# Handing a part of the row stores and relays of a long convolution from SyncE's queue to GpSimd's

## The chip, the cores and the metric

The kernel runs on one core of a Trainium2 chip. The metric is the device time of one execution in microseconds; the time before is 187.96 us, the median of three runs (187.35 to 188.18). All durations below come from one execution taken by the hardware profiler, whose span from the first to the last instruction is 187.3 us.

## The reference

Two independent heads read sequences of 2048 steps and 640 channels in bf16, and their results are laid side by side in an output of 2048 x 1280.

Head A is a diagonal complex state space model. Each channel pair turns x into 640 complex states by a matrix B, runs a recurrence over time, and maps back by a matrix C; a skip term x * Dskip is added:

```
h = Lam_bar * h + Bu[t]            # 2048 steps, 640 complex states
y = 2 * real(h @ C.T) + x * Dskip
```

Head B is a long convolution. k is first convolved with a kernel of 4 taps per channel and multiplied by v; the product kv is convolved over the whole sequence with a kernel of 2048 taps per channel, by Fourier transforms of length 4096; then a skip and a gate by q:

```
kv = conv4(k, shift_k) * v
y  = irfft(rfft(kv) * rfft(ssm_k))[:2048] + kv * ssm_D
out_B = q * y
```

## The kernel before

The program is a list of operations, each with the engines that may run it, a function that issues it, and the memory that it writes and reads. From those footprints `depend` (L92) finds what each operation must wait for. A long string, `ORDER` (L1117), fixes the rest: each entry such as `388S0` names operation 388, the engine that runs it (A ScalarE, V VectorE, G GpSimd, T TensorE, S SyncE), and a PSUM bank. `emit` (L122) issues the operations in that order; each engine runs its own in the order in which the string names them, and an operation at the head of an engine's queue that must wait holds all behind it. SyncE (SP) issues nearly all DMAs; ScalarE issues a few at the start; GpSimd issues none.

Head A works on TensorE with matmuls that fold 16 steps into one coarse step (L581, L602), a scan on VectorE (`coarse`, L656, with its multiplications on L679 and L682 to L690), matmuls that unfold again (L225 and L229, evicted on L726 and L728), and the map by C with the skip term (`project`, L732). The skip multiplies rows of x by `DR`, a copy of Dskip on all 128 partitions. `ld_Dr` (L372), which loads it, is the 91st operation; its first reader is `xd0` (L737).

Head B does its transforms as small matmuls. The channels are worked in five blocks of 128 for the short convolution, and in two halves of 320 for the long one. For block d:

- `load_kv` (L811) loads k and v of the block transposed, channels on partitions (L814). There is one k buffer (KT) for all five blocks, so `ld_k2` waits until the last tap of block 1 has read KT, `ld_k3` until the last tap of block 2, and so on; v has three buffers.
- `conv` (L827) multiplies k by the taps (L205 on VectorE, L206 on ScalarE), adds (L840) and multiplies by v (L841). All of blocks 0 to 2 but a few taps is on VectorE; the last product of block 3 is GpSimd's next work after the set-up tables.
- `plane` (L843) stores the 128 finished rows of 4096 bytes to a scratch tensor in DRAM, `kv_rows`: operations `pl0` to `pl4`.
- `relay` (L850) reads the rows of a half back with the 32 x 64 split of time that the transform needs. There are eight pieces a half, each of 40 channels: 32 partitions x 40 rows x 128 bytes, so 1280 separate runs of 128 bytes. A piece waits for the stores that hold its 40 channels.
- `s1` (L860, matmuls on L876 and L881, evicted on L886) is the first transform stage over the relayed rows; its units 0 to 4 read the four pieces of the first 40 columns, units 5 to 9 the other four. The second stage is on L900 and L913.

SP's order around the change is: the loads of k and v for blocks 0 and 1 and parts of x, the first load of C, `ld_k2`, `pl0`, `ld_v2`, a second load of C, `pl1`, `ld_k3`, the first piece, `pl2`, then the other seven pieces with two small loads among them, `ld_v3`, rows of x, `ld_k4`, a third part of C, the four loads of the second half's long kernel (L807), `ld_Dr`, and more rows of x.

Of the kernel before, what the change touches and what calls it, by code (L numbers as in the profile page):

```python
# [20 lines left out]
PACT, PDVE, PPOOL, PPE, PSP = "A", "V", "G", "T", "S"  # L21
# [336 lines left out]
def params(c):  # L358

    P, nc, v, f = c.P, c.nc, c.v, c.f  # L360
    V, G, A = PDVE, PPOOL, PACT
    lam_re, lam_im, ldt_in, dsk_in = c.ins["A_Lambda_re"], c.ins["A_Lambda_im"], c.ins["A_log_dt"], c.ins["A_Dskip"]
# [3 lines left out]
    for k, src in enumerate((lam_re, lam_im, ldt_in)):  # L366
        rows = pr[10 * k:10 * k + 10, :]
        P.add("ld_par", {PSP: .1, PACT: .1}, lambda e, rows=rows, src=src: e.dma_start(
            out=rows.rearrange("p (a b) -> p a b", a=2), in_=bass.AP(src.tensor, 0, [[64, 10], [0, 2], [1, 64]])),
            outs=[tk[:, k:k + 1]], ins=[pr], nbytes=2560)  # L370
    c.DR = v("DR")
    P.add("ld_Dr", {PSP: .1}, lambda e: e.dma_start(out=c.DR, in_=bass.AP(dsk_in.tensor, 0, [[0, 128], [1, 640]])), outs=[c.DR],  # L372
          nbytes=128 * 1280)
    PV = v("PV").bitcast(f32)
    g = P.group(1)
# [11 lines left out]
    for i, n in enumerate((1, 2, 4, 8, 16)):  # L387
        P.add("rn", {A: .2}, lambda e, i=i, n=n: e.activation(out=rn[:, i, :], in_=rho, func=FN.Exp, scale=float(n)),
              outs=[rn[:, i, :]], ins=[rho])
# [17 lines left out]
    for i in range(1, 4):  # L407
        P.add("fn", {G: .2}, lambda e, i=i: e.tensor_tensor(out=fn[:, i, :], in0=fn[:, i - 1, :], in1=fn[:, i - 1, :], op=ALU.add),
              outs=[fn[:, i, :]], ins=[fn[:, i - 1, :]])
    P.add("ph", {G: .4}, lambda e: e.tensor_tensor(  # L410
        out=ph.rearrange("p (x m) -> p x m", m=2), in0=bc(fn.rearrange("p n j -> p (n j)").rearrange("p (x o) -> p x o", o=1), [128, 40, 2]),
# [5 lines left out]
        out=al3, in0=al3, in1=bc(rn[:, 0:4, :].rearrange("p n j -> p (n j)").rearrange("p (x o) -> p x o", o=1), [128, 40, 2]), op=ALU.mult),  # L417
        outs=[al], ins=[al, rn[:, 0:4, :]])
# [4 lines left out]
    for lo, mi, val in ((0, 0, 1.0), (0, 1, 0.0), (64, 0, 0.0), (64, 1, 1.0)):  # L423
# [17 lines left out]
          outs=[t3(ga)[:, :, 0]], ins=[t3(ma)[:, :, 0], t3(mb)[:, :, 1]])  # L441
# [28 lines left out]
    for x in range(2):  # L470
# [5 lines left out]
              outs=[pc], ins=[ps, c30])  # L476
# [291 lines left out]
class PartB:  # L768
# [74 lines left out]
    def plane(self, d):  # L843

        c, P = self.c, self.c.P
        vt, tok = c.v("VT", 2048 * (d % 3), 2048), c.tok[:, d:d + 1]
        P.add(f"pl{d}", {PSP: 1.6}, lambda e: e.dma_start(out=c.kvdram[128 * d:128 * d + 128, :], in_=vt), outs=[tok], ins=[vt],
              nbytes=128 * 4096)

    def relay(self, hf):  # L850

        c, P = self.c, self.c.P
        for x, gh in [(x, gh) for gh in range(2) for x in range(4)]:
            lo = 320 * hf + 80 * x + 40 * gh
            dst = self.KV[32 * x:32 * x + 32, 40 * gh:40 * gh + 40]
            src = c.kvdram[lo:lo + 40, :].rearrange("n (a b) -> a n b", b=64)
            P.add(f"rl{hf}_{x}{gh}", {PSP: 1.2}, lambda e, dst=dst, src=src: e.dma_start(out=dst, in_=src), outs=[dst],
                  ins=[c.tok[:, lo // 128:(lo + 39) // 128 + 1]], nbytes=40 * 4096)

    def s1(self, what, hf, u):  # L860
# [237 lines left out]
def plain_order(P):  # L1098
# [16 lines left out]


ORDER = (  # L1117
# [40 lines left out]
)  # L1158


# [68 lines left out]
```

## Time and profile before

| what | value |
|---|---|
| median of three runs | 187.96 us |
| span of the profiled execution | 187.3 us |
| time of the runs less the span of the profile | about 0.7 us |
| TensorE (PE) busy | 175.6 us, 94% of the span |
| VectorE (DVE) busy | 158.0 us, 84% |
| ScalarE (ACT) busy | 147.7 us, 79% |
| GpSimd (POOL) busy | 72.6 us, 39% |
| granted TensorE clock | 0.999 |
| DMA | 30.15 MB in 106682 packets, 101274 of them under 512 bytes |

The profile's page does not print a time of the profiled execution beside its span; the sums below are made against the span of 187.3 us, and the 0.7 us around it are added at the end. In timeline rows the first number is the start in microseconds, the second the duration of the whole row, then the engine, the line and the operation, written and read tensor, shape, and the number of instructions merged into the row. Square brackets hold the idle time of that engine before the row and what ended it. An SP row lasts as long as SyncE needed to hand the DMA over, not until the data has landed.

### The profile page before, as it was taken

The numbers are of one execution on the slowest core, as the hardware profiler recorded it, in microseconds if no ns is written. First come the engines' busy times: TensorE is split into PE (matmuls) and PEld (weight loads), VectorE is DVE, ScalarE is ACT, GpSimd is POOL, SyncE is SP. The second block draws the span as 40 slices with busy tenths as digits, with TensorE's granted clock in tenths as the row PEclk, the third lists the DMA queues.
The fourth block names the chain that finished last, engine by engine and source line by source line (L and its number), as shares of the span: only waits on it lengthen the run. The fifth ranks groups of instructions, "written<-read, shape, count | busy, mean of one in ns | idle before, by whom it ended". The sixth has DMA issues, their size and how long they took to land.

```text
span 187.3 us, 7665 instructions
## 1 busy us (share of the span) xinstructions
PE 175.6 (94%) x3398; PEld 126.3 (67%) x3399; DVE 158.0 (84%) x225; ACT 147.7 (79%) x181; POOL 72.6 (39%) x68
## 2 busy tenths in 40 slices
PE   7998999999799979979997999999999999999992
PEld 2565666677468756656685688776588876887770
DVE  3537964679959899999969999899999999998961
ACT  2469699989899979999997997997898883985000
POOL 8679999900000000008803925730740000551620
PEclk9999999999999999999999999999999999999999
DMA  5999999799999989999989479402496993058996
GB/s 153 191 184 158 200 143 140 141 174 182 198 253 154 290 179 152 180 182 154 138 109 251 154 170 133 75 5 72 122 196 120 210 227 85 15 160 187 208 219 173
DMA packets 106682, 30.15 MB, mean 161 GB/s; under 512 B 101274, under 2 KB 106010, under 8 KB 106650
## 3 DMA queue, kind: packets, MB, share of 16 engines
q1 hardware_dynamic: 106332, 29.35, 86.7%
q8 instruction: 26, 0.43, 1.1%
q10 hardware_dynamic: 318, 0.33, 0.6%
q14 instruction: 6, 0.05, 0.1%
HBM read 11.32 MB, written 7.86 MB: 102 GB/s over the span
## 4 chain that ended last, share of the span: by engine, by line
PE 54%; DVE 23%; DMA 9%; ACT 8%; issue 3%; DVEq 0%; ACTq 0%
PE acc L225 17%; PE acc L581 13%; DMA arena<-in_B_k_dram 9%; PE acc L229 6%; DVE arena L728 6%; PE acc L900 6%; DVE arena L205 5%; ACT arena L913 5%; PE acc L951 4%; DVE arena L840 3%; PE acc L972 3%; PE acc L539 2%; DVE arena L754 2%; PE acc L881 1%; ACT arena L886 1%
## 5 line engine op out<-in xcount | busy, mean ns | idle before, releaser
L581 PE MATMUL acc<-arena 128*64 128x512 bf16 x400 | 45.6, 380 | 1.8 <-DVE arena L457 1.1
L913 ACT CAST arena<-acc 128x960 bf16<-128x960 f32 (+1 forms) x43 | 37.4, 916 | 4.0 <-PE acc L900 2.2
L225 PE MATMUL acc<-arena 128*128 128x320 bf16 (+2 forms) x255 | 36.4, 297 | 2.2 <-DVE arena L754 1.1
L581 PEld LDWEIGHTS <-arena 128*64 128x64 bf16 x400 | 26.0, 110 | 17.8 <-DVE arena L457 1.3
L886 ACT CAST arena<-acc 128x1024 bf16<-128x1024 f32 x37 | 35.8, 1034 | 2.1 <-PE acc L881 2.0
L225 PEld LDWEIGHTS <-arena 128*128 128x128 bf16 x256 | 23.7, 98 | 12.1 <-DVE arena L754 1.3
L841 POOL TENSOR_TENSOR arena<-arena 128x2048 bf16<-128x2048 bf16 x2 | 8.8, 4410 | 53.7 <-DVE arena L840 46.1
L900 PE MATMUL acc<-arena 128*64 128x160 bf16 x512 | 23.6, 235 | 1.8 <-DVE arena L679 1.4
L900 PEld LDWEIGHTS <-arena 128*64 128x64 bf16 x512 | 18.6, 110 | 8.3 <-ACT arena L913 2.2
L229 PE MATMUL acc<-arena 128*64 128x320 bf16 (+3 forms) x258 | 23.2, 313 | 0.5 <-DVE arena L690 0.5
L840 DVE TENSOR_TENSOR arena<-arena 128x2048 bf16<-128x2048 bf16 x14 | 17.6, 1256 | 4.5 <-ACT arena L206 4.3
L728 DVE TENSOR_TENSOR arena<-acc,arena 128x1024 bf16<-128x1024 f32 (+2 forms) x19 | 20.4, 1114 | 0.9 <-PE acc L229 0.5
L760 POOL TENSOR_TENSOR arena<-arena 128x640 bf16<-128x640 f32 x3 | 4.2, 1416 | 32.6 <-ACT arena L752 32.6
L956 ACT CAST arena<-acc 128x1024 bf16<-128x1024 f32 x16 | 15.4, 1025 | 1.7 <-PE acc L951 1.6
L229 PEld LDWEIGHTS <-arena 128*64 128x64 bf16 x258 | 13.0, 110 | 3.5 <-DVE arena L690 0.6
L876 PE MATMUL acc<-arena 128*64 128x128 bf16 x400 | 14.6, 220 | 0.2 <-ACT arena L886 0.2
L876 PEld LDWEIGHTS <-arena 128*64 128x64 bf16 x400 | 12.9, 110 | 2.4 <-ACT arena L886 0.9
L205 DVE TENSOR_SCALAR arena<-arena 128x2048 bf16<-128x2048 bf16 x15 | 11.0, 749 | 3.6 <-DMA arena<-in_B_k_dram 3.5
L754 DVE TENSOR_TENSOR arena<-acc,arena 128x640 bf16<-128x640 f32 x13 | 10.7, 820 | 3.5 <-PE acc L225 2.2
L206 ACT ACTIVATE arena<-arena 128x2048 bf16<-128x2048 bf16 (+2 forms) x10 | 11.1, 1112 | 1.5 <-DMA arena<-in_B_k_dram 1.5
L924 DVE TENSOR_TENSOR arena<-arena 128x2560 bf16<-128x2560 bf16 x8 | 11.9, 1484 | 0.1
L602 PE MATMUL acc<-arena 128*64 128x256 bf16 (+2 forms) x140 | 11.6, 291 | 0.1
(142 smaller groups left out, 284.4 us busy)
## 6 DMA issues: line engine op xcount, KB each, us to landing
out_dram<-arena SPq DMA_DIRECT2D x32, 160.0 KB, 3.3
arena<-in_B_ssm_k_dram SPq DMA_DIRECT2D x8, 320.0 KB, 6.1
kv_rows<-arena SPq DMA_DIRECT2D x5, 512.0 KB, 4.7
arena<-kv_rows SPq DMA_DIRECT2D x16, 160.0 KB, 4.0
arena<-in_A_x_dram SPq DMA_DIRECT2D x16, 160.0 KB, 3.5
arena<-in_B_q_dram SPq DMA_DIRECT2D x8, 320.0 KB, 6.3
arena<-in_A_B_im_dram ACTq DMA_DIRECT2D x1, 160.0 KB, 2.8
arena<-in_A_B_re_dram SPq DMA_DIRECT2D x1, 160.0 KB, 3.0
```

The lines of the kernel that those rows point to most:

```text
L205: vm = lambda e: lambda out, in_, by: e.tensor_scalar_mul(out=out, in0=in_, scalar1=by)
L225: e.matmul(out, lhsT=lhsT, rhs=rhs, start=start, stop=stop, skip_group_check=True)
L229: e.matmul(out[half], lhsT=lhsT[:, half], rhs=rhs, start=start, stop=stop, skip_group_check=True, tile_position=(0, 64 * r))
L581: e.matmul(o[64 * r:64 * r + 64], lhsT=self.BT[j][:, r, d, :], rhs=self.XP[:, d, 2 * q:2 * q + 2], start=(d == 0), stop=(d == 4), skip_gro ...
L728: e.tensor_tensor(out=o, in0=b, in1=o, op=ALU.add)
L754: e.tensor_tensor(out=two(ys), in0=two(B)[:, :, 0:320], in1=two(ys), op=ALU.add)
L840: P.add(f"ca{d}_{j}", tt, lambda e: e.tensor_tensor(out=t1, in0=t1, in1=t2, op=ALU.add), outs=[t1], ins=[t1, t2])
L876: e.matmul(B[64 * b:64 * b + 64, 128 * i:128 * i + 128], lhsT=lh[i], rhs=F[:, b, :], start=True, stop=True, tile_position=(0, 64 * b))
L886: P.add(f"e1{what}{hf}_{u}", {PACT: act(1024), PDVE: dve(1024)}, lambda e, B: c.CP[e](out=out, in_=(B.rearrange("p (l n s k) -> p k s l n" ...
L900: e.matmul(B[64 * s:64 * s + 64, 512 * b + 160 * i:512 * b + 160 * i + 160], lhsT=c.W[:, k, 64 * b:64 * b + 64], rhs=self.AS[hf][:, k, 160 ...
L913: c.CP[e](out=out, in_=b.rearrange("p r (k j n) -> p r k j n", k=n, j=4) if nj > 1 else b.rearrange("p r (k x) -> p r k x", k=n))
L956: P.add(f"er2{hf}_{u}", {PACT: act(1024), PDVE: dve(1024)}, lambda e, B: c.CP[e](out=out, in_=B.rearrange("p (s n b) -> p b s n", s=2, n=4 ...
```

## The change

Nine DMAs get GpSimd as their issuer: the stores `pl0` and `pl1` of the first two blocks, the load of Dskip `ld_Dr`, and six of the eight relay pieces of the first half (`rl0_00`, `rl0_01`, `rl0_10`, `rl0_11`, `rl0_20`, `rl0_21`). `pl2` and the two pieces that read block 2 (`rl0_30`, `rl0_31`) stay on SP. On GpSimd the nine stand between the last set-up product (84) and the last product of block 3 (453), in the order pl0, ld_Dr, pl1, rl0_00, rl0_01, rl0_10, rl0_11, rl0_20, rl0_21. In the string `388G0 91G0` stand right behind the end of block 0's convolution (387), and the other seven right behind the end of block 1's (398). The order of everything else, on every engine, is unchanged.

The diff, with the string cut to the entries that move:

```
-    P.add("ld_Dr", {PSP: .1}, ...
+    P.add("ld_Dr", {PSP: .1, PPOOL: .1}, ...
-        P.add(f"pl{d}", {PSP: 1.6}, ...
+        P.add(f"pl{d}", {PSP: 1.6, PPOOL: 1.6}, ...
-            P.add(f"rl{hf}_{x}{gh}", {PSP: 1.2}, ...
+            P.add(f"rl{hf}_{x}{gh}", {PSP: 1.2, PPOOL: 1.2}, ...
...
-  84G0 387V0 201T4 ... 400S0 ... 81A0 388S0 64V0 ... 398V0 199T0 ... 232A4 399S0 407V0
-  ... 243T6 411S0 207T0 ... 208A0 415S0 236A4 ... 414S0 ... 416S0 321V0 413S0 ... 412S0 ... 417S0 ... 91S0
+  84G0 387V0 388G0 91G0 201T4 ... 400S0 ... 81A0 64V0 ... 398V0 399G0 411G0 415G0 412G0 416G0 413G0 417G0 199T0
+  ... 232A4 407V0 ... 243T6 207T0 ... 208A0 236A4 ... 414S0 ... 321V0 ...
```

More of the change, by code (lines that the diff above doesn't have):

```diff
@@ L371, in params @@
     c.DR = v("DR")
-    P.add("ld_Dr", {PSP: .1}, lambda e: e.dma_start(out=c.DR, in_=bass.AP(dsk_in.tensor, 0, [[0, 128], [1, 640]])), outs=[c.DR],
+    P.add("ld_Dr", {PSP: .1, PPOOL: .1}, lambda e: e.dma_start(out=c.DR, in_=bass.AP(dsk_in.tensor, 0, [[0, 128], [1, 640]])), outs=[c.DR],
           nbytes=128 * 1280)
@@ L846, in plane @@
         vt, tok = c.v("VT", 2048 * (d % 3), 2048), c.tok[:, d:d + 1]
-        P.add(f"pl{d}", {PSP: 1.6}, lambda e: e.dma_start(out=c.kvdram[128 * d:128 * d + 128, :], in_=vt), outs=[tok], ins=[vt],
+        P.add(f"pl{d}", {PSP: 1.6, PPOOL: 1.6}, lambda e: e.dma_start(out=c.kvdram[128 * d:128 * d + 128, :], in_=vt), outs=[tok], ins=[vt],
               nbytes=128 * 4096)
@@ L856, in relay @@
             src = c.kvdram[lo:lo + 40, :].rearrange("n (a b) -> a n b", b=64)
-            P.add(f"rl{hf}_{x}{gh}", {PSP: 1.2}, lambda e, dst=dst, src=src: e.dma_start(out=dst, in_=src), outs=[dst],
+            P.add(f"rl{hf}_{x}{gh}", {PSP: 1.2, PPOOL: 1.2}, lambda e, dst=dst, src=src: e.dma_start(out=dst, in_=src), outs=[dst],
                   ins=[c.tok[:, lo // 128:(lo + 39) // 128 + 1]], nbytes=40 * 4096)
```

78 rows, old and new, of the table ORDER are left out of this document.

## The prediction

> **What bounds the kernel now.** I read the page first, then the chain of waits in order of time, then the timelines of SP, PE, DVE and POOL around the moved DMAs.
>
> ```profile
> span 187.3 us, 7665 instructions
> ...
> PE 175.6 (94%) x3398; PEld 126.3 (67%) x3399; DVE 158.0 (84%) x225; ACT 147.7 (79%) x181; POOL 72.6 (39%) x68
> ...
> DMA  5999999799999989999989479402496993058996
> ```
>
> PE is without work for 11.7 us of the span, so a change of issue can win little; it can lose much, since every engine runs a fixed order. The slices show the DMA engines nearly always busy from 5 to 100 us, which is where all nine moved DMAs lie. The chain, in order of time (start, duration):
>
> ```profile
> 34.99 6.07 DMA arena<-in_B_k_dram
> ...
> 48.18 5.76 DMA arena<-in_B_k_dram
> ...
> 59.81 5.37 DMA arena<-in_B_k_dram
> ...
> 65.20 1.42 DVE arena L205 x2
> 66.62 0.74 DVE arena L679
> ...
> 67.41 0.61 PE acc L900 x12
> ```
>
> Three of its links are flights of k (blocks 1, 2, 3): a k lands, DVE convolves it, the one k buffer comes free, the next k is issued. The last landing reaches PE by DVE's fixed order: two taps of block 3, then L679, which frees PE. PE and DVE show that as waits:
>
> ```profile
> 53.96 0.75 DVE L205 TENSOR_SCALAR arena<-arena 128x2048 bf16<-128x2048 bf16 x1 [1.90 <-DMA arena<-in_B_k_dram]
> ...
> 58.84 0.75 DVE L205 TENSOR_SCALAR arena<-arena 128x2048 bf16<-128x2048 bf16 x1
> ...
> 64.49 0.07 DVE L668 MEMSET arena<- 128x10 f32 x1
> 65.20 1.42 DVE L205 TENSOR_SCALAR arena<-arena 128x2048 bf16<-128x2048 bf16 x2 [0.65 <-DMA arena<-in_B_k_dram]
> ```
> ```profile
> 67.41 0.61 PE L900 MATMUL acc<-arena 128*64 128x160 bf16 x12 [1.39 <-DVE arena L679]
> ```
>
> **What SP shows.** Its queue over the same time:
>
> ```profile
> 48.18 2.14 SPq L814 DMA_TRANSPOSE arena<-in_B_k_dram  x1
> 50.37 0.58 SPq L847 DMA_DIRECT2D kv_rows<-arena  x1
> 51.00 3.93 SPq L814 DMA_TRANSPOSE arena<-in_B_v_dram  x1
> 54.97 3.23 SPq L556 DMA_TRANSPOSE arena<-in_A_C_im_dram  x1
> 58.30 1.40 SPq L847 DMA_DIRECT2D kv_rows<-arena  x1
> 59.81 3.06 SPq L814 DMA_TRANSPOSE arena<-in_B_k_dram  x1
> 63.04 0.46 SPq L857 DMA_DIRECT2D arena<-kv_rows  x1
> ...
> 67.63 3.23 SPq L857 DMA_DIRECT2D arena<-kv_rows  x4
> ...
> 72.74 1.86 SPq L857 DMA_DIRECT2D arena<-kv_rows  x2
> ...
> 77.68 0.53 SPq L736 DMA_DIRECT2D arena<-in_A_x_dram  x1
> ...
> 90.58 3.45 SPq L372 DMA_DIRECT2D arena<-in_A_Dskip_dram  x1
> ```
>
> SP is never free between 48.18 and 63.04, but equal stores take 0.58 and 1.40 us of it, and the load of Dskip, as large as a block of rows of x that takes 0.53, takes 3.45 behind four large loads. So an issue lasts not as long as its own work but until the engines have taken what stands ahead: SP is slow because the DMA engines are full. What the change takes off SP is then still to be carried by the same engines, and some of it earlier than now.
>
> **The change, part by part.**
>
> 1. The two stores. `pl0` waits for block 0's product, `pl1` for block 1's; the first ends at 37.89 + 1.23 = 39.12, the second at 50.83 + 1.23 = 52.06, and POOL has nothing to do from 37.88:
>
> ```profile
> 37.89 1.23 DVE L841 TENSOR_TENSOR arena<-arena 128x2048 bf16<-128x2048 bf16 x1 [1.83 <-DMA arena<-in_B_v_dram]
> ...
> 50.83 1.23 DVE L841 TENSOR_TENSOR arena<-arena 128x2048 bf16<-128x2048 bf16 x1
> ```
> ```profile
> 36.85 1.03 POOL L350 TENSOR_TENSOR arena<-arena 128x512 int32<-128x512 int32 x1
> 84.01 4.08 POOL L841 TENSOR_TENSOR arena<-arena 128x2048 bf16<-128x2048 bf16 x1 [46.12 <-DVE arena L840]
> ```
>
> They start some 11 and 6 us earlier than on SP. The pieces wait for them, and the v loads that reuse their buffers, on SP at 74.64 and 94.56, far behind. `pl0` (1.40 us of full engines) and `ld_Dr` (0.53) now run ahead of `ld_k2`: up to 1.9 us on its landing. The wait before 53.96 shows that DVE has no cover for that.
>
> 2. `ld_Dr`. It ends a wait. Its first reader, and PE behind it:
>
> ```profile
> 97.87 0.49 DVE L737 TENSOR_TENSOR arena<-arena 128x640 bf16<-128x640 bf16 x1 [1.38 <-DMA arena<-in_A_Dskip_dram]
> ```
> ```profile
> 99.37 0.85 PE L225 MATMUL acc<-arena 128*128 128x320 bf16 x5 [0.97 <-DVE arena L754]
> ```
>
> L754 needs that product, so PE's 0.97 us go: the one clear gain. The rows of x that L737 also reads were issued at 77.68. SP's later loads come up to 3.45 us sooner; no engine on the chain waits for them.
>
> 3. The six pieces. On SP one takes between 0.46 us (the row at 63.04) and 0.93 us (1.86 / 2), four together 3.23, so 0.81 each. The trace has no DMA issued by POOL, so the price there has to be bounded. Below: 0.46. Above: a piece is 1280 runs, each with a place to read and a place to write; at POOL's own price for a product of integers,
>
> ```profile
> 5.53 1.05 POOL L350 TENSOR_TENSOR arena<-arena 128x512 int32<-128x512 int32 x1
> ```
>
> 1.05 / 512 = 2.05 ns, that is 2 x 1280 x 2.05 ns = 5.2 us. I take the upper end: work of POOL is nearest to a row of POOL. The store has 128 runs, a tenth: 0.5 us.
>
> POOL then does the pieces from 52.06 + 0.5 = 52.6 on. `pl1` lands long before POOL reaches the piece that needs it (the third, at 63.0). The sixth is handed over at 52.6 + 6 x 5.2 = 83.8. It lands later than that; of the relay pieces on SP the quickest took 3.3 us from the start of its issue:
>
> ```profile
> DMA to landing us min/median/max: 3.3/4.0/4.9
> ```
>
> Less an issue of 0.46 that is 2.8 us; so 86.6. Who needs it:
>
> ```profile
> 77.13 0.44 PE L881 MATMUL acc<-arena 64*64 64x64 bf16 x32
> ...
> 78.65 0.64 PE L876 MATMUL acc<-arena 128*64 128x128 bf16 x16
> 80.09 0.22 PE L225 MATMUL acc<-arena 128*128 128x128 bf16 x1 [0.81 <-ACT arena L886]
> ```
>
> These are the first two units of the transform (2 and 6). Unit 2 needs the fifth piece (81.4 by the same sum, 4.2 late), unit 6 the sixth: PE, in its fixed order, stands until 86.6 instead of 78.65, 8.0 us. Behind it the 0.81 us at 80.09 (ACT evicting unit 2) fall into that stand. The crowding of part 1, less than these 8.0 us and ahead of them on the same PE, is swallowed too. POOL's own next work, the product at 84.01, is only just held by pieces done at 83.8; its result is stored on SP at 100.36, so 12 us cover it.
>
> Sum: 187.3 + 8.0 - 0.81 - 0.97 = 193.5 us of span, and with the 0.7 us around it 194.2 (against the median of 187.96).
>
> Point from which this decides: pieces cheaper than (78.65 - 2.8 - 52.6) / 6 = 3.9 us land in time.
>
> [...]
>
> **The rivals.**
>
> *Crowding: pieces are quick* (0.46 to 3.9 us). Then all six and `ld_Dr` are carried before `ld_k3` lands: 6 x 0.81 + 0.53 = 5.4 us newly ahead of it, on engines that are full. The two taps at 65.20 and L679 behind them start that much later, PE waits 5.4 us more at 67.41, and 0.97 come back: 191.7 of span, 192.4. For it: the three waits on k. Against: breaks in the transposes may take some of it.
>
> *Room: faster.* The DMA engines fit a second queue between the first one's packets and the pieces are quick. `ld_k3` has no store of 1.40 us ahead of it and lands by so much sooner, but DVE comes to it at 64.49 + 0.07 = 64.56, so only 0.64 us of its 0.65 count; with 0.97 from Dskip 1.6: 185.7 of span, 186.4. For it: SP's full queue. Against: the slices of 9.
>
> *Balance.* Quick pieces with most of the crowding hidden: a loss of about 1 us on k and a gain of 0.97 on Dskip leave 188.
>
> *A lock between DVE and POOL.* Where the two work at once, both are slow in this trace:
>
> ```profile
> 32.66 3.02 POOL L350 TENSOR_TENSOR arena<-arena 128x512 int32<-128x512 int32 x2
> ```
> ```profile
> 32.33 1.45 DVE L840 TENSOR_TENSOR arena<-arena 128x2048 bf16<-128x2048 bf16 x1 [2.52 <-ACT arena L206]
> ```
>
> POOL's pair took 1.51 us each where one takes 1.05, and DVE's sum 1.45. If DVE's taps stop POOL while they run, the pieces lose what lies between 52.6 and 83.8:
>
> ```profile
> 52.60:83.80 31.20, 5.92 (x8) 1.00 1.05 204
> ```
>
> 5.9 us more on the same wait: 194.2 + 5.9 = 200.1. [...]
>
> *Slow pieces.* At twice the price, 10.4 us, the sixth lands at 52.6 + 62.4 + 2.8 = 117.8: 39.2 - 1.8 = 37.4 us more, 225.
>
> That POOL's order does not do what it says (a store handed over later than its data) would need a wait there that I do not find: between 37.88 and 84.01 nothing else is on that queue.
>
> **How the numbers follow.** Forecast 0.34, its own range 190.6 to 199 (pieces of 4.6 us: 83.0 - 78.65 - 1.8 = 2.6 more; of 6: 91.4 - 78.65 - 1.8 = 11.0 more). Crowding 0.25, lock 0.13, slow pieces 0.08: slower 0.80. Room 0.13: faster. Balance 0.07: within 0.5%, which is about what a measurement of this kernel can tell from no change. The range goes from 186.0 (most of room) to 211 (pieces of 8 us: 52.6 + 48 + 2.8 = 103.4, 23 more); it leaves out slow pieces and the rims of room and lock, under 2 in 10.
>
> **What would show it.** Right: POOL with six long rows of about 5 us each from 52.6 on; a wait of PE of some 8 us ahead of L881 and L876, put down to the DMA arena<-kv_rows; no wait of DVE for Dskip. Crowding: short rows on POOL and longer waits of L205 for in_B_k. Lock: POOL's rows longer where L205 runs. Room: k landing sooner than 5.4 us after its issue. I am wrong if no wait for kv_rows or in_B_k has grown.

## The result

The changed kernel takes 200.34 us in the median of four runs (200.09 to 203.42), the kernel before on the same chip 188.07 us (187.35 to 190.49): 1.0651 times as long, with an interval of 1.0619 to 1.0683. That is 12.3 us slower. The forecast was 194.2 us, slower, within 186.0 to 211. The ratios, here and below, compare only those executions of each kernel that lie within 1.5% of its fastest one, so a ratio can be smaller than that of the medians. The direction and the range held; the mechanism held to be likeliest did not occur. Another one of the list, crowding, did: it was priced at 5.4 us ahead of L900, and 9.65 us came.

The page of the changed kernel (columns as in the page of before; the last rows are DMA issues with KB each and the median time to landing):

```profile
span 198.4 us, 7676 instructions
...
PEclk9999999999999855799999999999999999999999
DMA  5999999999999996745999728920369798038895
...
q1 hardware_dynamic: 98124, 27.15, 76.5%
q0 software_dynamic: 720, 2.20, 6.5%
...
arena<-kv_rows POOLq DMA_DIRECT2D x6, 160.0 KB, 11.0
```

The queue q0 is new: it is GpSimd's, with 2.20 MB in 720 packets, 3 KB each in the mean. SyncE's q1 has 277 bytes a packet. A piece handed over by GpSimd lands after 11.0 us in the median; before, on SP, after 4.0. The profiled run took 200.16 us, so 1.8 us lie around the span, not the 0.7 that the prediction took.

GpSimd's timeline (an issue row lasts as long as GpSimd needed):

```profile
39.67 1.07 POOL L847 DMA_DIRECT2D kv_rows<-arena  x1
40.74 0.67 POOL L372 DMA_DIRECT2D arena<-in_A_Dskip_dram  x1
51.08 0.54 POOL L847 DMA_DIRECT2D kv_rows<-arena  x1 [9.67 <-DVE arena L841]
51.66 2.96 POOL L857 DMA_DIRECT2D arena<-kv_rows  x3
55.67 2.82 POOL L857 DMA_DIRECT2D arena<-kv_rows  x3 [1.04 <-DMA kv_rows<-arena]
```

A piece costs GpSimd 0.94 to 0.99 us, in the mean of three. The last is handed over at 58.5, where the prediction had 83.8. SyncE's timeline over the same time:

```profile
48.32 2.79 SPq L814 DMA_TRANSPOSE arena<-in_B_k_dram  x1
51.16 3.98 SPq L814 DMA_TRANSPOSE arena<-in_B_v_dram  x1
55.23 7.32 SPq L556 DMA_TRANSPOSE arena<-in_A_C_im_dram  x1
62.65 8.74 SPq L814 DMA_TRANSPOSE arena<-in_B_k_dram  x1
```

Although two stores and a piece are gone from this stretch of the queue, SP is later. The hand-over of C_im, 3.23 us before, takes 7.32, that of `ld_k3` 8.74 against 3.06. The chain of waits (start, duration) gives the flight of k3 and what it releases:

```profile
62.65 12.18 DMA arena<-in_B_k_dram
74.85 1.42 DVE arena L205 x2
76.27 0.74 DVE arena L679
```

VectorE and TensorE, from their timelines:

```profile
53.40 0.76 DVE L205 TENSOR_SCALAR arena<-arena 128x2048 bf16<-128x2048 bf16 x1 [2.62 <-DMA arena<-in_B_k_dram]
...
74.85 1.42 DVE L205 TENSOR_SCALAR arena<-arena 128x2048 bf16<-128x2048 bf16 x2 [9.70 <-DMA arena<-in_B_k_dram]
```
```profile
77.06 1.01 PE L900 MATMUL acc<-arena 128*64 128x160 bf16 x12 [11.82 <-DVE arena L679]
78.21 1.89 PE L900 MATMUL acc<-arena 128*64 128x160 bf16 x24
79.88 3.28 PE L581 MATMUL acc<-arena 128*64 128x512 bf16 x20
...
91.95 0.22 PE L225 MATMUL acc<-arena 128*128 128x128 bf16 x1 [0.79 <-ACT arena L886]
```

So TensorE stands still for 11.82 us where it stood for 1.39, on the same chain: k3, two taps, L679. The account of the two spans:

- k3 is handed over 62.65 - 59.81 = 2.84 us later and flies 12.18 - 5.37 = 6.81 us longer. Together 9.65, which is by how much L900 starts later (77.06 against 67.41).
- Behind the stand the same matmuls are slow: 24 of L900 take 1.89 us against 1.03, 20 of L581 take 3.28 against 2.33. From L900 to L225 it is 14.89 us, before 80.09 - 67.41 = 12.68: 2.21 more.
- The 0.97 us ahead of L225 behind Dskip are gone.

That is 10.89 of the 11.1 us between the spans (198.4 - 187.3). The medians lie 12.3 apart. With 1.8 us around its span the profiled execution of before would have taken some 189.1 us (an estimate), about 1.1 above its median, and it had a late start of about that size. Its first taps of block 1 start at 41.15, those of the changed kernel at 39.88:

```profile
41.15 1.42 DVE L205 TENSOR_SCALAR arena<-arena 128x2048 bf16<-128x2048 bf16 x2 [0.90 <-DMA arena<-in_B_k_dram]
```

So where traces are compared below, the start of that L900 is counted from these taps: 67.41 - 41.15 = 26.26 before, 77.06 - 39.88 = 37.18 after, 10.92 later.

The share of time, clock and bytes in windows (engines PE, PEld, DVE, ACT, POOL with busy time; then the granted clock, the DMA share and GB/s), first of before, then of after:

```profile
58.00:66.00 8.00, 7.91 (x148) 6.27 (x142) 7.28 (x10) 7.57 (x16) 0.00 (x0) 1.00 1.16 240
```
```profile
58.00:66.00 8.00, 7.24 (x128) 5.70 (x126) 6.20 (x8) 7.57 (x15) 0.48 (x1) 1.00 1.20 115
66.00:74.00 8.00, 0.00 (x0) 0.00 (x0) 0.00 (x0) 0.47 (x1) 0.00 (x0) 0.63 1.21 112
```

The DMA engines are as full as before and move less than half the bytes. TensorE's granted clock falls while it stands, to 0.63 in the mean of 66 to 74 us.

### The profile page after: what moved, and what is told of

The parts are those of the page before. It is cut to its first block, busy times and chain, and to the rows that moved or that the text cites. A ratio compares the mean times of both kernels' runs of the same rounds, so it can differ in the third digit from the quotient of the medians.

```text
span 198.4 us, 7676 instructions
## 1 busy us (share of the span) xinstructions
PE 177.9 (90%) x3398; PEld 126.3 (64%) x3399; DVE 161.6 (81%) x225; ACT 147.5 (74%) x181; POOL 83.0 (42%) x77
## 4 chain that ended last, share of the span: by engine, by line
PE 33%; DMA 20%; DVE 18%; ACT 13%; SPq 10%; issue 4%; DVEq 0%; ACTq 0%
PE acc L225 15%; DMA arena<-in_B_k_dram 11%; DMA arena<-in_B_v_dram 5%; PE acc L900 5%; PE acc L229 4%; ACT arena L913 4%; PE acc L951 4%; DVE arena L728 4%; SPq L547 4%; DVE arena L840 3%; SPq L807 3%; ACT arena L206 3%; DMA arena<-in_A_x_dram 3%; PE acc L972 3%; SPq L512 2%
## 5 line engine op out<-in xcount | busy, mean ns | idle before, releaser
L581 PE MATMUL acc<-arena 128*64 128x512 bf16 x400 | 46.5, 385 | 0.4 <-DMA arena<-in_A_B_im_dram 0.2
L225 PE MATMUL acc<-arena 128*128 128x320 bf16 (+2 forms) x255 | 36.3, 297 | 1.4 <-ACT arena L886 0.8
L581 PEld LDWEIGHTS <-arena 128*64 128x64 bf16 x400 | 25.0, 112 | 18.3 <-issue 2.1
L900 PE MATMUL acc<-arena 128*64 128x160 bf16 x512 | 24.9, 243 | 12.2 <-DVE arena L679 11.8
L900 PEld LDWEIGHTS <-arena 128*64 128x64 bf16 x512 | 19.7, 114 | 18.7 <-DVE arena L679 12.0
L225 PEld LDWEIGHTS <-arena 128*128 128x128 bf16 x256 | 23.8, 98 | 11.2 <-ACT arena L575 0.7
L841 POOL TENSOR_TENSOR arena<-arena 128x2048 bf16<-128x2048 bf16 x2 | 9.3, 4664 | 43.7 <-DVE arena L840 43.7
L205 DVE TENSOR_SCALAR arena<-arena 128x2048 bf16<-128x2048 bf16 x15 | 11.2, 761 | 12.5 <-DMA arena<-in_B_k_dram 12.3
L840 DVE TENSOR_TENSOR arena<-arena 128x2048 bf16<-128x2048 bf16 x14 | 18.8, 1342 | 2.3 <-ACT arena L206 2.1
L648 ACT CAST arena<-acc 128x256 bf16<-128x256 f32 (+1 forms) x14 | 6.4, 478 | 14.0 <-PE acc L602 14.0
L206 ACT ACTIVATE arena<-arena 128x2048 bf16<-128x2048 bf16 (+2 forms) x10 | 11.1, 1112 | 1.4 <-DMA arena<-in_B_k_dram 1.0
```

Source lines behind the costliest of these rows:

```text
L206: self.SM = {nc.scalar: lambda out, in_, by: nc.scalar.mul(out, in_, by), nc.vector: vm(nc.vector), nc.gpsimd: vm(nc.gpsimd)}
L225: e.matmul(out, lhsT=lhsT, rhs=rhs, start=start, stop=stop, skip_group_check=True)
L581: e.matmul(o[64 * r:64 * r + 64], lhsT=self.BT[j][:, r, d, :], rhs=self.XP[:, d, 2 * q:2 * q + 2], start=(d == 0), stop=(d == 4), skip_gro ...
L840: P.add(f"ca{d}_{j}", tt, lambda e: e.tensor_tensor(out=t1, in0=t1, in1=t2, op=ALU.add), outs=[t1], ins=[t1, t2])
L900: e.matmul(B[64 * s:64 * s + 64, 512 * b + 160 * i:512 * b + 160 * i + 160], lhsT=c.W[:, k, 64 * b:64 * b + 64], rhs=self.AS[hf][:, k, 160 ...
```

## The experiments

Kernels that use GpSimd's queue in this stretch scatter by several per cent from execution to execution (186.27 to 195.53 us in the first one below), so where a profiled execution is far from the median its own time is given. The interval of a ratio is against the kernel before on the same chip.

### Which part of the change costs: pieces, stores, Dskip

**The six pieces back on SP, stores and Dskip on GpSimd.**

```
- 388G0 91G0 ... 399G0 411G0 415G0 412G0 416G0 413G0 417G0 ...
+ 388G0 91G0 ... 399G0 ... 444S0 ... 411S0 ... 415S0 ... (the pieces as before)
```

> The six relay pieces go back to their old places on SyncE; the two stores and the load of Dskip stay on GpSimd. Theory 'mixing' (the pieces' transfers from GpSimd's queue and SyncE's transposes slow each other while both are in flight): the wait for the k of block 3, 9.70 us in the changed kernel, falls under 2 us, the time comes back to 187 to 189. Theory 'stores' (the two stores and Dskip, run early beside SyncE's loads, are what holds up k): still 195 or more. With mixing, the 0.97 us of Dskip may show as a gain, unless the stores take it back.

Measured: 191.83 us (186.27 to 195.53), before 187.55; ratio 1.0009, 0.9952 to 1.0066. The profiled run, of 190.41 us, is not one of the quick ones, and shows k2 late:

```profile
54.67 0.76 DVE L205 TENSOR_SCALAR arena<-arena 128x2048 bf16<-128x2048 bf16 x1 [4.94 <-DMA arena<-in_B_k_dram]
```

Without the pieces there are executions as quick as before. What the stores and Dskip cost is not a steady price: it runs from nothing to 8 us, from one execution to the next, and in this one it is a wait for k2. That wait comes back in the profiled runs below, and it has to be kept apart from what the pieces do. With the stores on SP it is 1.90 (before) to 2.35 us, and 3.16 with Dskip alone on GpSimd. With the stores and Dskip on GpSimd it is 2.62 in the changed kernel and 4.94 to 7.53 in the seven other kernels.

**Only the six pieces on GpSimd.**

```
- 388G0 91G0 ... 399G0 411G0 ...
+ ... 388S0 ... 399S0 411G0 ... (91S0 as before)
```

> Only the six pieces go to GpSimd; stores and Dskip are on SyncE as before. The pieces now wait for stores that land near 55 and 63 us. Mixing: the three pieces of the second store run beside the flight of the k of block 3 (issued near 60), which then takes over 8 us instead of 5.4, and the time is 193 to 199. Stores: no more than 189.

Measured: 190.48 us, before 187.55; 1.0174, 1.0117 to 1.0231. The stores are on SP again, so three pieces have no data until `pl1` has been written, and GpSimd's timeline shows that these go out only when `ld_k3` has been handed over (58.45 to 63.23):

```profile
53.99 2.86 POOL L857 DMA_DIRECT2D arena<-kv_rows  x3 [14.94 <-DMA kv_rows<-arena]
63.70 2.76 POOL L857 DMA_DIRECT2D arena<-kv_rows  x3 [6.86 <-DMA kv_rows<-arena]
```

TensorE waits 2.58 us ahead of L900, which starts 28.54 us behind the taps, 2.3 later than before. So the parts do not add up: 0.1% and 1.7% alone, 6.5% together. In the changed kernel all six pieces are out ahead of k3, because the stores that they wait for go early too.

**Two pieces, the stores and Dskip on GpSimd.**

```
- ... 411G0 415G0 412G0 416G0 413G0 417G0
+ ... 411G0 415G0 (the other four on SP as before)
```

> As the changed kernel, but four of the six pieces go back to SyncE; GpSimd issues two, near 52 us. Mixing with a loss that grows with each piece: about a third of the excess, 190 to 193. Were the loss the sum of their bytes alone, 2 x 0.81 us on the way of k, 189 at most. If a threshold decides (the last three pieces, which ran beside the flight of the k of block 3), 187 to 188.5.

Measured: 194.21 us (190.26 to 195.19), before 187.46; the scatter allows no ratio. In a profiled run of 195.19 us the hand-overs of v2 and C_im take 6.07 and 5.85 us, and L900 starts 32.56 behind the taps, 6.3 later. Of the 6.3 us, 3.65 are VectorE's longer wait for k2 (5.55 against 1.90); k3's later hand-over behind its last tap and its flight of 5.84 us make the rest. So two early pieces together with the stores cost more than half of what the whole change costs, and most of it is at k2, where a wait of 4.94 came without any piece.

**Only Dskip on GpSimd.**

```
- 388G0 91G0 ... 399G0 411G0 415G0 412G0 416G0 413G0 417G0
+ 91G0 (all others on SP as before)
```

> The kernel before with only the load of Dskip on GpSimd. The wait of 1.38 us of DVE and of 0.97 us of PE near 98 go; nothing else moves, except that 0.53 us of transfers stand in the way of SyncE's loads near 41 us. Gain: 0 to 1 us, ratio 0.995 to 1.000.

Measured: 188.21 us, before 187.46; 1.0043, 1.0007 to 1.0079. TensorE's wait ahead of L225 is gone, and two others are longer, that of VectorE for k2 (1.90 before) and that of TensorE ahead of L900 (1.39 before):

```profile
53.38 0.76 DVE L205 TENSOR_SCALAR arena<-arena 128x2048 bf16<-128x2048 bf16 x1 [3.16 <-DMA arena<-in_B_k_dram]
```
```profile
66.99 0.60 PE L900 MATMUL acc<-arena 128*64 128x160 bf16 x12 [1.83 <-DVE arena L679]
```

L900 starts 27.66 behind the taps, 1.4 later: one load of 160 KB takes back at k2 and k3 more than the 0.97 us that it wins.

### Queue or order: the same pieces early, from other engines

**The pieces on SP, right ahead of `ld_k3`.**

```
- 399G0 411G0 415G0 412G0 416G0 413G0 417G0 ... 444S0
+ 399G0 ... 411S0 415S0 412S0 416S0 413S0 417S0 444S0
```

> The six pieces on SyncE, but as early as on GpSimd: right ahead of the load of k of block 3; stores and Dskip on GpSimd. Theory 'work ahead' (what counts is only that the pieces' transfers stand ahead of that k, by whatever queue): as slow as the changed kernel, 198 or more. Mixing: in one queue the pieces cost their own 6 x 0.81 = 4.9 us and no more, k of block 3 lands some 5 us late, no loss of clock in proportion: 191 to 194.

The stores and Dskip stay on GpSimd. Measured: 195.38 us, before 187.55; 1.0438, 1.0375 to 1.0502. VectorE, SP, then TensorE:

```profile
54.98 0.76 DVE L205 TENSOR_SCALAR arena<-arena 128x2048 bf16<-128x2048 bf16 x1 [5.17 <-DMA arena<-in_B_k_dram]
```
```profile
57.31 6.71 SPq L857 DMA_DIRECT2D arena<-kv_rows  x6
64.12 4.16 SPq L814 DMA_TRANSPOSE arena<-in_B_k_dram  x1
```
```profile
72.45 1.01 PE L900 MATMUL acc<-arena 128*64 128x160 bf16 x12 [7.64 <-DVE arena L679]
```

L900 is 7.3 us later from the taps, and the pieces make only part of it. The wait for k2 (5.17 against 1.90) is 3.3 us of the 7.3. The pieces take 6.71 us of SP ahead of k3, so k3 goes out at 64.12, 3.5 us behind its last tap (0.2 before): 3.3 more. Its flight of 6.11 us is 0.7 longer. So pieces early on SP cost 4.0 us at k3. In the changed kernel the same two terms, hand-over behind the last tap (59.21 to 62.65) and flight, are 10.0 us longer than before.

**The pieces handed over by ScalarE at the same places.** The page calls ScalarE's queue `hardware_dynamic`, as it does SyncE's.

```
- ... 411G0 415G0 412G0 416G0 413G0 417G0
+ ... 411A0 415A0 412A0 ... 416A0 413A0 417A0
```

> The six pieces are issued by ScalarE (another hardware queue) at about the times at which GpSimd issued them. If any second queue beside SyncE's transposes gives the loss, the flight of the k of block 3 is again over 9 us and the time 198 or more. If it is GpSimd's own packets (4096 bytes that hold 32 runs of 128), then packets of 128 bytes on ScalarE's queue take turns with the transposes' 256, the flight is near 7 to 9 us, and the time 191 to 196, in which up to 4 us may be ScalarE's own time for the issues.

Measured: 194.01 us, before 187.55; 1.0339, 1.027 to 1.0408. Here k3 lands 5.8 us after its hand-over, and VectorE waits only 0.18 us for it; for k2, with the stores and Dskip on GpSimd, it waits 7.53. By the median of its six pieces, 7.3 us from issue to landing, the last three, issued from 57.42, 57.83 and 59.30 on, were still in flight when k3 went out at 62.99 (an estimate). ScalarE's timeline shows it held by its own hand-overs, and TensorE waits behind it; the last line is ScalarE's queue on the page:

```profile
50.64 4.71 ACTq L857 DMA_DIRECT2D arena<-kv_rows  x2
...
59.30 3.04 ACTq L857 DMA_DIRECT2D arena<-kv_rows  x1
```
```profile
56.68 0.64 PE L876 MATMUL acc<-arena 128*64 128x128 bf16 x16 [3.54 <-ACT arena L886]
64.12 1.72 PE L602 MATMUL acc<-arena 128*64 128x256 bf16 x28 [1.41 <-ACT arena L648]
```
```profile
q10 hardware_dynamic: 8094, 1.31, 4.6%
```

Over 52 to 70 us this kernel moves 230 GB/s, the changed one 159, the one before 225. So here the same early pieces from ScalarE's queue slow neither the rate nor k3. They hold up the engine that issues them instead, as they do on SP. Whether they slowed k2 is open: it landed 8.7 us after its hand-over began, beside the first three pieces, but in the next kernel it took 8.6 with no piece in flight. In the kernel before, that queue had 318 packets and 0.6%; the six pieces are the other 7776 packets, 126 bytes each in the mean, and some 4.0% of 16 engines' 191.5 us, which is 123 us, or 16 ns a packet.

**The pieces on GpSimd, but held until a tap of block 3 is done.**

```
+ c.P.ops[411].preds.add(446)
- 399G0 411G0 ...    + 399G0 ... 446V0 411G0 415G0 412G0 416G0 413G0 417G0
```

> As the changed kernel (nine DMAs on GpSimd), but GpSimd's first piece waits until a tap of block 3 has been computed, that is, until the k of block 3 has landed. Theory 'mixing': with the pieces out of its way that k lands within 6 us of its issue again, the long wait for it falls from 9.7 us to under 3, and the time to 187 to 190, though the pieces now land late in the seventies and may hold the transform (PE at 77 to 79) for a microsecond or two. If GpSimd's pieces were bad by themselves (late landings of 11 us wherever they run), PE waits for them and the time stays over 193.

Measured: 195.62 us, before 187.46; 1.0363, 1.0297 to 1.0429. The expected 187 to 190 us missed. The profiled run, of 200.8 us, is well above the median. In it, with no piece beside it, k3 is handed over in 2.05 us and has landed when VectorE comes to its taps at 70.12, 4.84 us after the start of the hand-over (a flight of 5.37 before). But k2 had come late with the stores and Dskip on GpSimd (VectorE waits 7.18 us), and the late pieces become the wait that the likeliest case foretold:

```profile
65.28 2.05 SPq L814 DMA_TRANSPOSE arena<-in_B_k_dram  x1
...
81.06 8.83 SPq L814 DMA_TRANSPOSE arena<-in_B_k_dram  x1
```
```profile
88.29 0.64 PE L881 MATMUL acc<-arena 64*64 64x64 bf16 x32 [3.82 <-DMA arena<-kv_rows]
```

The second SP row is `ld_k4`, which now has the pieces beside it: its hand-over took 8.83 us, that of k3 2.05. In this run the slowing goes where the pieces go.

### What it is in GpSimd's DMAs: six copies that nobody waits for

Two kernels leave the kernel before as it was, on SP, and add six copies of 160 KB from GpSimd's queue, one with runs of 128 bytes, one with whole rows of 4096. They go from DRAM into a spare tensor in DRAM, where the pieces go to the on-chip memory. The code is shortened; `d` stands for rows of the spare tensor.

```
+ for x, gh in ((0, 0), (0, 1), (1, 0), (1, 1), (2, 0), (2, 1)):
+     lo = 80 * (2 * x + gh)
+     s = ssm_k[lo:lo + 80:2, :].rearrange("n (a b) -> a n b", b=64)    # runs; rows: without the rearrange
+     P.add("junk", {PPOOL: 1.2}, dma_start(out=d, in_=s))               # behind 398, block 1's product
```

> The kernel before, with all its DMAs on SyncE as they were, and six more DMAs that nobody waits for: GpSimd copies, from the end of block 1's product (52.06), six times 160 KB of ssm_k to a spare tensor in DRAM, in 1280 runs of 128 bytes each, like the pieces. Theory (runs of 128 bytes from GpSimd's queue and SyncE's transposes hinder each other): the issues of ld_v2 and C_im on SyncE stretch to 4 us and over 6 us, k3 flies 8 to 12 us and not 5.37, TensorE's L900 behind the second taps of block 3 starts at 72 to 77 and not 67.41: 193 to 200. Rival (the two queues only share the engines, by bytes): 0.96 MB at the 229 GB/s of this stretch are 4.3 us, k3 lands at most so much later: 189 to 192.5, and the kernel with long rows is within 1 us of this one.

> As the kernel with six spare copies, but each of the six takes its 160 KB in 40 whole rows of 4096 bytes. Theory (it is the short runs that hinder): SyncE's issues and k3's flight stay near those of before, at most the 4.3 us of the bytes later: 188 to 191, and at least 3 us under the kernel with short runs. Rival (it is GpSimd's queue, whatever the runs): as slow as with short runs, 193 to 200. Rival (bytes alone): both kernels at 189 to 192.5.

Measured, before 186.84 us: short runs 196.08 us, ratio 1.0485 (1.0444 to 1.0526); whole rows 193.4 us (189.99 to 194.51, too scattered for a ratio, its profiled run 189.99). GpSimd's queue on the two pages, short runs first:

```profile
q0 software_dynamic: 384, 0.98, 3.2%
```
```profile
q0 software_dynamic: 384, 0.98, 1.4%
```

Equal bytes in equally many packets, some 2.5 KB each in the mean, but 3.2% of 16 engines' 194.2 us are 99 us, 259 ns a packet in the mean, and 1.4% of 188.2 are 42 us, 110 ns a packet. Spread over 16 engines, that is 6.2 and 2.6 us of each engine. SP's row of k3 and TensorE, short runs and then rows:

```profile
59.11 7.45 SPq L814 DMA_TRANSPOSE arena<-in_B_k_dram  x1
...
72.33 1.01 PE L900 MATMUL acc<-arena 128*64 128x160 bf16 x12 [7.72 <-DVE arena L679]
```
```profile
58.33 4.91 SPq L814 DMA_TRANSPOSE arena<-in_B_k_dram  x1
...
67.61 0.61 PE L900 MATMUL acc<-arena 128*64 128x160 bf16 x12 [2.76 <-DVE arena L679]
68.23 1.55 PE L900 MATMUL acc<-arena 128*64 128x160 bf16 x24
```

From hand-over to landing k3 takes 11.00 and 7.05 us (5.37 before). L900 starts 33.49 and 28.71 us behind the taps, 7.2 and 2.5 later than before. So six copies that nobody waits for, on GpSimd's queue, are enough to double the flight of k3, and with short runs they cost more than their bytes: 0.98 MB at 229 GB/s would be 4.3 us, and all four runs are 8.2 to 9.8 us above before. This much is shown.

What it is in those copies is not. The profiled run with whole rows came out as the theory of the short runs had it, but it is the fastest of four; the other three (193.21 to 194.51) are 3 to 4.5 us above it, and by the median the rival, GpSimd's queue whatever the runs, came true (193 to 200). The engine time that the copies take in all does not set the price either: ScalarE's six pieces took 123 us, more than the 99 here, and k3 flew 5.8 us behind and beside them. One difference between the two is how long a packet holds an engine, 259 ns against 16. That this is the cause is argued, not shown: who was served when, inside a DMA engine, no view here tells.

### The load that stands ahead of k3, and the clock

**The changed kernel with C_im put behind `ld_k3`.**

```
- 400S0 ... 401S0 ... 271S0 ... 444S0
+ 400S0 ... 401S0 ... 444S0 271S0
```

> The changed kernel, with the one transposing load that stood between ld_v2 and ld_k3 (C_im, whose hand-over took 7.32 us there) put behind ld_k3. Theory (whatever is in flight beside the pieces is slow): k3 is handed over as soon as its buffer is free, near 59.2 and not 62.65, still beside the pieces, and flies 9 to 12 us: it lands at 68 to 71.5 and the time is 194 to 197. Rival (the transposes only queue behind each other, and the pieces cost them little): with C_im away k3 flies 5.4 to 6 us and lands at 65: 188 to 190.5. Rival (C_im's own reader is late next and takes it back): k3 lands sooner, but the time stays at 199 to 200.5.

Measured: 198.84 us (195.28 to 201.63, again too scattered for a ratio). In the profiled run of 195.28 us, the fastest, k3 is handed over hardly earlier, at 62.48, since VectorE had waited for k2 and its last tap of block 2, at 61.70, ended when k3 went out:

```profile
56.64 0.75 DVE L205 TENSOR_SCALAR arena<-arena 128x2048 bf16<-128x2048 bf16 x1 [6.54 <-DMA arena<-in_B_k_dram]
...
61.70 0.75 DVE L205 TENSOR_SCALAR arena<-arena 128x2048 bf16<-128x2048 bf16 x1
```

k3 then flies 7.62 us. The expectations had k3 out at 59.2, and that failed; L900 is 6.9 us later from the taps. Of these, 4.6 are the longer wait for k2 and 2.3 k3's longer flight. So with C_im out of the way k3 is late all the same, but hand-over and flight of k3 lost 10.0 us in the changed kernel and 2.3 here: C_im's stretched hand-over is not cleared, and its share stays open.

**The changed kernel with 50 matmuls that nobody reads, ahead of the stand.** They keep TensorE busy while it would have stood. The code shows only the function that issues them.

```
+ def keep(e, B):
+     for _ in range(50):
+         e.matmul(B[:, 0:512], lhsT=c.I3[:, 0:128], rhs=bc(c.I3[:, 0:1], [128, 512]), start=True, stop=True)
```

> The changed kernel with 50 matmuls of 512 columns that nothing reads, put on PE ahead of the work that waits 11.8 us; they keep PE busy through the stand. Theory 'clock': of the loss some 2 us are PE and its granted clock at half behind the stand (24 matmuls of L900 in 1.89 us against 1.03), so the clock stays 1.0 and the time falls by about 2 us to 198. Without it: no change, or slower by what the extra matmuls overhang.

Measured: 208.4 us, before 187.46; 1.0997, 1.0904 to 1.1089. TensorE behind the filler:

```profile
67.83 11.06 PE L1099 MATMUL acc<-arena 128*128 128x512 bf16 x50
80.50 0.61 PE L900 MATMUL acc<-arena 128*64 128x160 bf16 x12 [1.60 <-DVE arena L679]
...
81.12 1.03 PE L900 MATMUL acc<-arena 128*64 128x160 bf16 x24
81.98 2.33 PE L581 MATMUL acc<-arena 128*64 128x512 bf16 x20
```

The matmuls have their durations of before again, 1.03 and 2.33 us. In the changed kernel, with 1.89 and 3.28, the granted clock was 0.50 from 68.2 to 81.7. Here its mean over the span of 208.0 us is 0.982, a loss of 3.7 us, and the windows from 160 us on (0.99, 0.84, 1.00, 0.89) have all of that, so behind the filler it was full (an estimate). So the 2.2 us behind the stand are a matter of the clock. As a whole the kernel is slower, and the expected 198 us missed. In the profiled run, of 209.79 us, k3 came later still: VectorE waits 5.44 us for k2 (2.62 in the changed kernel), 4.06 for the v of block 2 (0.89) and 6.24 for k3, whose taps start at 78.29 (74.85). TensorE also stood twice near the end of the span, ahead of L972 and put down to issue: 2.34 us up to 169.27 and 2.97 up to 190.77, with a granted clock of 0.84 over 170 to 180 us and 0.89 over 190 to 208. The cause of those stands is open.

### A version that should have won

The kernel before, with Dskip loaded ahead of the long kernel's four loads and `pl1` behind `ld_k3`, all on SP:

```
- ... 399S0 ... 444S0 ... 729S0 ... (91S0 behind the loads of the long kernel)
+ ... 444S0 399S0 ... 729S0 91S0 ...
```

> All nine DMAs are SyncE's again. Against the kernel before, only two change place in SyncE's queue: the load of Dskip goes from behind the four loads of the long kernel to a place ahead of them (it then lands long before 97.87, where its reader waited 1.38 us), and the store pl1 goes from just ahead of ld_k3 to just behind it. Theory (no second queue in play, the gains are only those of the two waits): the 0.97 us of TensorE ahead of L225 at 99.37 go; ld_k3 is handed over up to 1.40 us sooner, of which VectorE can use 0.64; together at most 1.6 us: 186.4 to 187.4. Rival (a load of Dskip taken earlier delays what TensorE needs next as much as it saves, and pl1 holds back the fourth piece): 187.6 to 188.5.

Measured: 188.18 us, before 186.84; 1.0053, 1.0021 to 1.0085. The theory fell. The waits at L900 and for Dskip are gone from its trace, but another stands in the place of the second:

```profile
97.03 1.00 PE L881 MATMUL acc<-arena 64*64 64x64 bf16 x96 [1.62 <-DVE arena L809]
```

L809 adds to the long kernel and waits for the four loads that now stand behind Dskip. No version tried beats the kernel before.

## Why the prediction was right and wrong

**The bound** was read rightly: k lands, DVE convolves, k3 reaches TensorE through two taps and L679. All the loss in the trace goes down that chain.

**Part 1, the stores.** "Up to 1.9 us" on k2: the wait ahead of the taps of block 2 grew from 1.90 to 2.62, 0.72 us, within the bound. In the other kernels with these stores and Dskip on GpSimd the same wait was 4.94 to 7.53, outside it. The sentence that `pl1` lands long before it is needed is wrong: GpSimd waited 1.04 us for it (its row at 55.67), ahead of the fourth piece, not the third. No engine waited for that piece.

**Part 2, Dskip.** The 0.97 us went, as said. But "the one clear gain" was not one: alone on GpSimd the load cost more at k2 and k3, and taken early on SP it only handed its wait to L809.

**Part 3, the pieces: the step that failed.** The price of 5.2 us a piece on GpSimd was taken from its arithmetic and from the upper of two bounds. It measured 0.94 to 0.99, about twice the lower bound of 0.46 and far below the deciding point of 3.9 us. With it fell the stand of 8.0 us ahead of units 2 and 6: TensorE has no wait for kv_rows; the last piece is issued at 57.6, and none takes more than 14.1 us to land. GpSimd's queue and the DMA engines behind it were taken as one row of work; the trace shows a quick hand-over, under 1 us, and a slow flight, 11.0 us in the median. The range held because its upper cases reached that far, not because of the sum; that the result lies on the forecast's side and inside the range is luck as far as the sum goes, since another mechanism brought it there.

**Crowding was the mechanism, and its term was mis-sized.** It had 5.4 us more at L900 and 192.4 us in all. Measured: 9.65 there. Both signs that the prediction gave for it came, short rows of GpSimd and longer waits of L205. The pieces on SP ahead of k3, a kernel without a piece on GpSimd's queue, cost 4.0 us at k3, near the 4.9 of six times 0.81. In the changed kernel hand-over and flight of k3 cost 10.0. Two things were missing. On GpSimd's queue the pieces cost more than their 0.81 us on SP, and SP's hand-overs stretch meanwhile; the six spare copies show that traffic on that queue does this, and why a packet of it should do so stays open. And behind the stand of 11.82 us TensorE's clock was low: 2.21 us more, which no case of the prediction had.

**The other rivals.** Room, the one that would have been faster, is out: bytes per time halved (240 to 115 GB/s over 58 to 66 us). So is balance. The lock: its 200.1 us lies next to the measured 200.34, but by coincidence. GpSimd's rows are short beside VectorE's taps, 0.94 to 0.99 us a piece, so it did not decide; that the two equal stores took 1.07 and 0.54 us is left open.

## What to carry to other kernels

When a DMA is given to a second queue, price what it does to the transfers in flight beside it, by the one that the critical chain waits for; here the time of the issuing instruction, under 1 us a piece, said nothing of that. Where the DMA engines are already full, an earlier start of a transfer that is not urgent can be a later landing of one that is: here a transpose suffered beside GpSimd's queue (11.00 and 12.18 us instead of 5.37), and hardly beside the same pieces on ScalarE's (5.8). When a unit's price is bounded from far apart, put the likeliest case where the mechanism beyond the deciding point is, or give both nearly equal chances.

## What was not expected of the hardware

- GpSimd's queue packs runs of 128 bytes: 384 packets for 0.98 MB, 259 ns each in the mean, against 110 ns for the same bytes in rows of 4096. ScalarE's queue carried such runs in packets of 126 bytes, 16 ns each.
- In one execution, a single load of 160 KB on that queue, issued at 39.12, went with a hand-over of C_re on SP of 5.66 us instead of 3.10 and a wait of VectorE for k2 of 3.16 instead of 1.90.
- TensorE came back slow behind long stands, but the length alone does not decide: 24 matmuls of L900 took 1.03 us behind stands of 2.58 and 2.65 us, 1.55 behind one of 2.76, 1.89 behind 6.64, 7.64 and 11.82. Behind the stand of 2.34 us in the kernel with 50 spare matmuls, shorter than two that cost nothing, 40 matmuls of L225 took 7.28 us where twice 20 ahead of it took 2.89 each, and the granted clock was 0.84 over 170 to 180 us. What decides is open.
- The same program with stores on GpSimd's queue ran between 186.27 and 195.53 us on one chip, while the kernel before, beside it, ran between 186.0 and 189.94. Why the flights differ so much from execution to execution is open.
